# Batch 0 of a fused attention and MLP kernel: deferred pair sums, smaller last chunks, weights cast by their loads, the next batch's loads right behind them

## The chip, the cores and the metric

The kernel runs on one core of one Trainium2 chip. The metric is the device time of one execution in microseconds (us), as the median of several runs. A profiled execution spans some 2 us less than the time measured for it (772.4 against 774.1 for the kernel before); positions in time are from the start of that span. A load or a transpose has landed when the last of its 16 semaphore updates has come; all landings below are read from the trace's records of these updates.

## The reference

Four batches of q, k and v, each 6080 x 256 in fp32, tau = 1, then an MLP from 256 to 2048 and back:

```python
qn = q / (norm(q, axis=1) + 1e-06);  kn = k / (norm(k, axis=1) + 1e-06)
s = kn.transpose(0, 2, 1) @ qn / tau            # 256 x 256 for each batch
a = softmax(s)
x = (v @ a).reshape(B * N, 256)
out = gelu_tanh(x @ w_in) @ w_out               # w_in 256 x 2048, w_out 2048 x 256
```

Because `a` is small, the kernel multiplies it with w_in first (`aw`). A block of 512 rows of v then needs two products: `hp = aw^T v^T`, gelu, and `yp = g^T w_out`. Each batch has 12 blocks. While batch b's blocks run, the Gram matrix of batch b+1 is fed between them. Batch 0 has nothing to hide behind: its q and k come first, as fp32, and are cast and squared on chip.

## The kernel before

The order of the loads after batch 0's q and k, with the helpers that matter (cuts marked):

```python
first_chunks = chunks_of([2, 4, 6, 6, 6, 6, 6, 6, 3, 2])     # slots of 128 rows
for n, ch in enumerate(first_chunks):
    ...
    nc.vector.tensor_copy(qkb, st);  nc.scalar.activation(sqb, st, AF.Square)
    nc.vector.tensor_add(pair[:, :, 0:h], sqb[:, :, 0:h], sqb[:, :, h : 2 * h])
    ... gram(...), col_sums(...)
    stage_chunk(n + 4)
    if n == len(first_chunks) - 1:
        nc.gpsimd.tensor_copy(gate[:, 0:1], st[0:1, 1, 0, 0:1])   # GpSimd's loads wait here
...
def turn_v(nb):                       # v is needed transposed
    ...
    for s in range(n):
        nc.sync.dma_start_transpose(out=vT[:, :, s * 128 : s * 128 + 128], in_=t[:, s, :])
load_v(1)                             # GpSimd load, casts fp32 to bf16
for half in range(2):                 # w_in: fp32 by SyncE, cast on GpSimd
    ...
    nc.sync.dma_start(out=w[...], in_=win_v[...])
    nc.gpsimd.tensor_copy(win_bf[...], w[...])
for half in range(2):                 # w_out: likewise
    ...
for nb in (2, 3):
    load_v(nb)
...
# inside the loop over blocks
turn_v(nb + 2); load_v(nb + 4)
# on the first step of a batch's block 0: chunks 0 to 2 of the next batch, casting loads by GpSimd
```

In this text, v1 is block 1 of v in batch 0, and chunk (1,0) is the first chunk of q and k of batch 1.

Of the kernel before, what the change touches and what calls it, by code (L numbers as in the profile page):

```python
# [8 lines left out]
FP32 = mybir.dt.float32  # L9
# [9 lines left out]
def kernel(  # L19
# [10 lines left out]
    nc = tc.nc  # L30
# [13 lines left out]
    const = ctx.enter_context(tc.tile_pool(name="const", bufs=1))  # L44
    stage = ctx.enter_context(tc.tile_pool(name="stage", bufs=4))
    qkp = ctx.enter_context(tc.tile_pool(name="qkp", bufs=4))
    sqp = ctx.enter_context(tc.tile_pool(name="sqp", bufs=2))
    sq1 = ctx.enter_context(tc.tile_pool(name="sq1", bufs=4))
    accp = ctx.enter_context(tc.tile_pool(name="accp", bufs=2))
    smx = ctx.enter_context(tc.tile_pool(name="smx", bufs=2))  # L50
    awp = ctx.enter_context(tc.tile_pool(name="awp", bufs=2))
    vts = ctx.enter_context(tc.tile_pool(name="vts", bufs=4))
    gp = ctx.enter_context(tc.tile_pool(name="gp", bufs=2))
    yout = ctx.enter_context(tc.tile_pool(name="yout", bufs=3))
    vin = ctx.enter_context(tc.tile_pool(name="vin", bufs=5))

    pA = ctx.enter_context(tc.tile_pool(name="pA", bufs=2, space=bass.MemoryType.PSUM))
# [6 lines left out]



    def chunks_of(sizes):
        found, s0 = [], 0
        for n, size in enumerate(sizes):
            found.append((s0, size, n == 0))  # L70
            s0 += size
        assert s0 == S_ALL
        return found

    def load_chunk(eng, dst, b, chunk):
        s0, size, rem = chunk
        for x, src in enumerate((q, k)):
            eng.dma_start(  # L78
                out=dst[:, x, 0:size, :],
                in_=src[b, s0 * 128 : (s0 + size) * 128, :].rearrange("(p s) c -> p s c", s=size))  # L80
        if rem:
            for x, src in enumerate((q, k)):
                eng.dma_start(out=dst[:REM, x, size, :], in_=src[b, S_ALL * 128 : N, :])

    def slots_of(chunk):
        _, size, rem = chunk
        return [(s, 128) for s in range(size)] + ([(size, REM)] if rem else [])

    n_all = S_ALL + 1


    first_chunks = chunks_of([2, 4, 6, 6, 6, 6, 6, 6, 3, 2])
    staged = []

    def stage_chunk(n):
        if n < len(first_chunks):
            st = stage.tile([128, 2, SMAX, 256], FP32, tag="st", name="st")
            load_chunk(nc.sync, st, 0, first_chunks[n])
            staged.append(st)

    for n in range(4):
# [30 lines left out]
    def col_sums(cols, x, ones, first, last):  # L132

        for m in range(4):
            nc.tensor.matmul(  # L135
                cols[:, m : m + 1],
                lhsT=x[:, m // 2, m % 2 * 128 : m % 2 * 128 + 128],
                rhs=ones,
                start=first and m == 0,
                stop=last,  # L140
                skip_group_check=True,
            )
# [51 lines left out]

    G = pA.tile([128, 2, 256], FP32, tag="a", name="G")
    cols = pA.tile([128, 512], FP32, tag="a", name="cols")
    seen = 0
    for n, ch in enumerate(first_chunks):
        st = staged[n]
        size = ch[1]  # L200
        qkb = qkp.tile([128, 2, SMAX, 256], BF16, tag="qk", name="qkb")
        sqb = sqp.tile([128, 2, SMAX, 256], BF16, tag="sq", name="sqb")
        pair = sqp.tile([128, 2, SMAX // 2, 256], BF16, tag="pair", name="pair")
        for lo, hi, rows in [(0, size, 128)] + ([(size, size + 1, REM)] if ch[2] else []):
            nc.vector.tensor_copy(qkb[:rows, :, lo:hi], st[:rows, :, lo:hi])  # L205
            nc.scalar.activation(sqb[:rows, :, lo:hi], st[:rows, :, lo:hi], AF.Square)  # L206
        h = size // 2
        nc.vector.tensor_add(pair[:, :, 0:h], sqb[:, :, 0:h], sqb[:, :, h : 2 * h])  # L208
        for s, rows in slots_of(ch):
            gram(G, qkb, s, rows, seen == 0, seen == n_all - 1)  # L210
            seen += 1
        parts = [pair[:, :, s, :] for s in range(h)]
        if size % 2:
            parts.append(sqb[:, :, size - 1, :])
        if ch[2]:
            parts.append(sqb[:REM, :, size, :])
        for m, x in enumerate(parts):
            col_sums(cols, x, ones_bf[: x.shape[0], :],
                     n == 0 and m == 0, n == len(first_chunks) - 1 and m == len(parts) - 1)
        stage_chunk(n + 4)  # L220
        if n == len(first_chunks) - 1:
            nc.gpsimd.tensor_copy(gate[:, 0:1], st[0:1, 1, 0, 0:1])

    v0 = stage.tile([128, 2, SMAX, 256], FP32, tag="st", name="v0")
# [11 lines left out]
    def load_v(nb):  # L236
        if nb >= B * n_blocks:
            return
        r0, n, rest = v_parts(nb)
        t = vin.tile([128, 4, 256], BF16, tag="v", name="vb")  # L240
        nc.gpsimd.dma_start(  # L241
            out=t[:, 0:n, :],
            in_=v_rows[r0 : r0 + n * 128, :].rearrange("(p s) c -> p s c", s=n))
        if rest:
            nc.gpsimd.dma_start(out=t[:rest, n, :], in_=v_rows[r0 + n * 128 : r0 + n * 128 + rest, :])
        v_of[nb] = t

    def turn_v(nb):
# [8 lines left out]
            nc.sync.dma_start_transpose(out=vT[:, :, n * 128 : n * 128 + rest], in_=t[:rest, n, :])  # L257
        vT_of[nb] = vT

    load_v(1)  # L260

    def flat_stage(n, shape):
        w = stage.tile([128, 2, SMAX, 256], FP32, tag="st", name="wst")
        return w.rearrange("p a b c -> p (a b c)")[:, 0:2048].rearrange("p (c d) -> p c d", c=n)

    for half in range(2):
        w = flat_stage(2, None)
        for x in range(2):
            c0 = half * 1024 + x * 512
            nc.sync.dma_start(out=w[:, :, x * 512 : x * 512 + 512], in_=win_v[:, :, c0 : c0 + 512])  # L270
            nc.gpsimd.tensor_copy(win_bf[:, :, c0 : c0 + 512], w[:, :, x * 512 : x * 512 + 512])
    for half in range(2):
        w = flat_stage(8, None)
        nc.sync.dma_start(out=w, in_=wout_v[:, half * 8 : half * 8 + 8, :])
        nc.gpsimd.tensor_copy(wout_bf[:, half * 8 : half * 8 + 8, :], w)  # L275
    for nb in (2, 3):
        load_v(nb)


    r = smx.tile([128, 4], FP32, tag="r", name="r")  # L280
# [1 line left out]
    nc.scalar.activation(dummy, ones_f, AF.Exp)  # L282
    norms(r)
    Gs = scaled(G, r)
    vT0 = vts.tile([128, 2, 512], BF16, tag="vT", name="vT")
    vps = []
    for cc in range(2):
        p = pY.tile([128, 2, 256], FP32, tag="y", name="vps").rearrange("p a b -> p (a b)")
        for s in range(4):
            nc.tensor.matmul(p[:, s * 128 : s * 128 + 128],  # L290
                             lhsT=v0[:, s, cc * 128 : cc * 128 + 128],
                             rhs=ident, is_transpose=True)
        vps.append(p)
    T = turned(Gs)
    nc.scalar.activation(vT0[:, 0, :], vps[0], AF.Copy)
    nc.vector.tensor_copy(vT0[:, 1, :], vps[1])
    eT = smx.tile([128, 2, 256], BF16, tag="eT", name="eT")
    for jc in range(2):
        nc.scalar.activation(eT[:, jc, :], T[:, jc, :], AF.Exp, scale=r[:, jc : jc + 1])
    nc.scalar.activation(dummy, ones_f, AF.Gelu_apprx_tanh)  # L300
    rsinv = row_sums(eT)
    aw = awp.tile([128, 2, D], BF16, tag="aw", name="aw")
    wide = pH.tile([128, 2, 512], FP32, tag="h", name="wide")
    for ic in range(2):
        aw_part(eT, rsinv, aw, 0, ic, ps=wide[:, ic, :], act=ic == 1)
    aw_left = [(fs, ic) for fs in range(1, 4) for ic in range(2)]

    def more_aw(n):
        for _ in range(n):
            if aw_left:  # L310
                aw_part(eT, rsinv, aw, *aw_left.pop(0))

    more_aw(2)

    vT_of[0] = vT0
    turn_v(1)

    later_chunks = chunks_of([5, 6, 6, 6, 6, 6, 6, 6])

    def attention_steps(b, aw_next):  # L320

        loaded = []

        def load(n):
            if n < len(later_chunks):
                t = qkp.tile([128, 2, SMAX, 256], BF16, tag="qk", name="qkb")
                load_chunk(nc.gpsimd, t, b, later_chunks[n])
                loaded.append(t)

        for n in range(3):  # L330
            load(n)
        for _ in range(10):
            yield
        G = pA.tile([128, 2, 256], FP32, tag="a", name="G")
        acc = accp.tile([128, 2, 256], FP32, tag="acc", name="acc")
        seen = 0
        for n, ch in enumerate(later_chunks):
            load(n + 3)
            for s, rows in slots_of(ch):
                first, last = seen == 0, seen == n_all - 1  # L340
                gram(G, loaded[n], s, rows, first, last)
                flat = loaded[n][:rows, :, s, :]
                if first:
                    nc.vector.tensor_mul(acc, flat, flat)
                else:
                    sq = sq1.tile([128, 2, 256], BF16, tag="sq", name="sq")
                    nc.vector.tensor_mul(sq[:rows], flat, flat)  # L347
                    nc.vector.tensor_add(acc[:rows], acc[:rows], sq[:rows])  # L348
                seen += 1
                yield  # L350
                if seen % 4 == 0:
                    yield
# [42 lines left out]
    def y_part(st, s, fc0, fc1):  # L395
# [16 lines left out]
        if fc1 < FC:  # L412
            return
        if s == 0:
            st["ysb"] = yout.tile([128, 4, 256], FP32, tag="ysb", name="ysb")
        ysb = st["ysb"]
        r0 = b * N + blk * BLK
        if not (s % 2 == 1 or s == len(rows_of) - 1 or alone):
# [91 lines left out]
```

## Time and profile before

| | before |
|---|---|
| time, median of 3 runs | 774.2 us |
| TensorE busy | 740.1 us, 96% |
| last column sum of batch 0 ends | 39.0 us |
| block 0 starts (first `hp` product) | 46.0 us |
| block 1, block 2 start | 56.1, 79.1 us |
| TensorE waits over 0.3 us from block 1 on | 4.49 at chunk (1,0), 0.74 at block 2 |

The page's slices show TensorE full after the first tenth. The chain of waits tells which early event set the end, the timeline tells how long TensorE stood before an instruction and for whom (in square brackets), and the view of the DMA queues counts packets: q0 holds the loads that cast (GpSimd issues them), q1 the plain loads, stores and transposes. The lines themselves are in the prediction.

### The profile page before, as it was taken

To read this page: it belongs to the slowest core of one execution; us is meant where nothing else is said; L and a number is where in the kernel's file an instruction comes from. 1 tells how busy PE (TensorE), PEld (TensorE's weight loads), DVE (VectorE), ACT (ScalarE), POOL (GpSimd) and SP (SyncE) were. 2 spreads that over 40 slices of the span, in tenths; PEclk is the share of its full clock that TensorE was granted. 3 is DMA by queue.
4 is the path that set the end of the run, shared out by engine and by line. 5 is a ranking of instruction groups with operands and counts; after the bars stand their busy time and mean duration, and the time that the engine had idled before them with its cause. 6 is when DMAs were issued, how large, how long until landed. Compare 5 with 4: busy or idle time off the path is not lost.

```text
span 772.4 us, 12183 instructions
## 1 busy us (share of the span) xinstructions
PE 740.1 (96%) x5135; PEld 507.4 (66%) x5220; DVE 279.1 (36%) x485; ACT 421.3 (55%) x412; POOL 68.9 (9%) x121
## 2 busy tenths in 40 slices
PE   4787999999999999999999999999999999999998
PEld 2544666667666666667666666666667666666666
DVE  4732545453511555454431354545351101110011
ACT  5673555555555555555555555555545555555552
POOL 0052011001210002000300010100100000000000
PEclk9998999999999999999999999999999999999999
DMA  8999878323983466811794167732433333212111
GB/s 342 361 227 198 148 139 148 63 63 71 178 124 82 90 109 110 146 45 42 136 167 102 38 136 136 124 65 70 85 69 81 67 69 89 60 52 73 40 56 52
DMA packets 81751, 85.95 MB, mean 111 GB/s; under 512 B 56608, under 2 KB 60192, under 8 KB 81696
## 3 DMA queue, kind: packets, MB, share of 16 engines
q1 hardware_dynamic: 67216, 54.29, 25.8%
q0 software_dynamic: 14480, 30.87, 24.4%
q8 instruction: 41, 0.67, 0.4%
q14 instruction: 14, 0.11, 0.0%
HBM read 78.91 MB, written 24.90 MB: 134 GB/s over the span
## 4 chain that ended last, share of the span: by engine, by line
PE 88%; DMA 7%; ACT 1%; SPq 1%; issue 1%; POOL 0%; DVE 0%; ACTq 0%; POOLq 0%
PE yp L407 43%; PE hp L458 40%; PE G L123 4%; DMA st<-in_k_dram 3%; DMA vT<-vb 2%; DMA wst<-in_moe_w_out_dram 2%; ACT sqb L206 1%; PE ps L183 1%; SPq L255 1%; POOL wout_bf L275 0%; DMA vb<-in_v_dram 0%; SPq L78 0%; PE cols L135 0%; ACT g L462 0%; PE T L161 0%
## 5 line engine op out<-in xcount | busy, mean ns | idle before, releaser
L462 ACT ACTIVATE g<-hp 128x1024 bf16<-128x1024 f32 (+1 forms) x384 | 389.6, 1015 | 323.6 <-PE hp L458 314.9
L407 PE MATMUL yp<-wout_bf,g 128*128 128x256 bf16 (+1 forms) x3072 | 397.9, 273 | 0.7
L458 PE MATMUL hp<-vT,aw 128*128 128x512 bf16 (+1 forms) x1458 | 386.1, 378 | 5.0 <-DMA vT<-vb 0.7
L407 PEld LDWEIGHTS <-g 128*128 128x128 bf16 (+1 forms) x3072 | 301.2, 98 | 114.7 <-issue 3.3
L458 PEld LDWEIGHTS <-aw 128*128 128x128 bf16 x1536 | 150.1, 98 | 109.4 <-issue 6.2
L423 DVE COPY ysb<-yp 128x512 f32<-128x512 f32 (+1 forms) x93 | 64.0, 689 | 390.8 <-PE yp L407 390.8
L348 DVE TENSOR_TENSOR acc<-acc,sq 128x512 f32<-128x512 f32 (+1 forms) x141 | 97.6, 692 | 4.8
L123 PE MATMUL G<-qkb 128*128 128x256 bf16 (+1 forms) x384 | 75.6, 302 | 20.1 <-DVE qkb L205 15.7
L123 PEld LDWEIGHTS <-qkb 128*128 128x128 bf16 (+1 forms) x384 | 39.6, 107 | 29.2 <-DVE qkb L205 16.7
L347 DVE TENSOR_TENSOR sq<-qkb 128x512 bf16<-128x512 bf16 (+1 forms) x141 | 58.8, 417 | 0.0
L241 POOL DMA_DIRECT2D vb<-in_v_dram x47 | 26.2, 559 | 207.4 <-DMA vT<-vb 205.6
L192 DVE TENSOR_SCALAR aw<-ps,rsinv 128x512 bf16<-128x512 f32 x30 | 22.5, 750 | 29.0 <-PE ps L183 23.9
L78 POOL DMA_DIRECT2D qkb<-in_q_dram x24 | 13.2, 552 | 196.0 <-PE G L123 113.7
L206 ACT ACTIVATE sqb<-st 128x3072 bf16<-128x3072 f32 (+4 forms) x11 | 22.5, 2062 | 12.9 <-DMA st<-in_k_dram 8.8
L205 DVE CAST qkb<-st 128x3072 bf16<-128x3072 f32 (+4 forms) x11 | 14.6, 1330 | 8.7 <-DMA st<-in_k_dram 8.6
L183 PE MATMUL ps<-win_bf,eT 128*128 128x512 bf16 x54 | 17.3, 398 | 0.1
L358 POOL TENSOR_TENSOR r<-r,half 128x4 f32<-128x4 f32 x3 | 3.1, 1037 | 141.8 <-DVE r L357 141.8
L78 POOL DMA_DIRECT2D qkb<-in_k_dram x24 | 13.3, 555 | 1.4 <-DMA vb<-in_v_dram 1.4
L383 DVE RECIPROCAL den<-den 128x256 f32<-128x256 f32 x6 | 10.5, 1752 | 0.2
L427 DVE COPY ysb<-yp 64x256 f32<-64x256 f32 (+1 forms) x7 | 2.7, 415 | 21.2 <-PE yp L407 21.2
L208 DVE TENSOR_TENSOR pair<-sqb 128x1536 bf16<-128x1536 bf16 (+2 forms) x10 | 7.7, 767 | 7.0 <-ACT sqb L206 7.0
L183 PEld LDWEIGHTS <-eT 128*128 128x128 bf16 x64 | 6.2, 101 | 3.8 <-issue 1.9
(50 smaller groups left out, 63.4 us busy)
## 6 DMA issues: line engine op xcount, KB each, us to landing
out_dram<-ysb SPq DMA_DIRECT2D x44, 512.0 KB, 3.0
vb<-in_v_dram POOLq DMA_DIRECT2D x43, 256.0 KB, 5.5
qkb<-in_q_dram POOLq DMA_DIRECT2D x21, 384.0 KB, 6.1
qkb<-in_k_dram POOLq DMA_DIRECT2D x21, 384.0 KB, 7.7
st<-in_q_dram SPq DMA_DIRECT2D x6, 768.0 KB, 10.9
st<-in_k_dram SPq DMA_DIRECT2D x6, 768.0 KB, 13.0
vT<-vb SPq DMA_TRANSPOSE x188, 3.8
wst<-in_moe_w_in_dram SPq DMA_DIRECT2D x4, 512.0 KB, 6.5
```

What stands on the lines that cost most here:

```text
L78: eng.dma_start(out=dst[:, x, 0:size, :], in_=src[b, s0 * 128 : (s0 + size) * 128, :].rearrange("(p s) c -> p s c", s=size))
L123: nc.tensor.matmul(G[:, ic, :], lhsT=qk[:rows, 1, s, ic * 128 : ic * 128 + 128], rhs=qk[:rows, 0, s, :], start=first and ic == 0, stop=las ...
L183: nc.tensor.matmul(ps, lhsT=eT[:, jc, ic * 128 : ic * 128 + 128], rhs=win_bf[:, jc, fs * 512 : fs * 512 + 512], start=jc == 0, stop=jc == 1)
L192: nc.vector.tensor_scalar_mul(dst, ps, scale)
L206: nc.scalar.activation(sqb[:rows, :, lo:hi], st[:rows, :, lo:hi], AF.Square)
L241: nc.gpsimd.dma_start(out=t[:, 0:n, :], in_=v_rows[r0 : r0 + n * 128, :].rearrange("(p s) c -> p s c", s=n))
L347: nc.vector.tensor_mul(sq[:rows], flat, flat)
L348: nc.vector.tensor_add(acc[:rows], acc[:rows], sq[:rows])
L407: nc.tensor.matmul(yp[:rows, at, :], lhsT=g[:, fc, s * 128 : s * 128 + rows], rhs=wout_bf[:, fc, :], start=fc == 0, stop=fc == FC - 1)
L423: nc.vector.tensor_copy(ysb[:, s0 : s + 1, :], yp[:, 0 : s + 1 - s0, :])
L458: nc.tensor.matmul(hp[:, j, :cols], lhsT=aw[:, cc, fc * 128 : fc * 128 + 128], rhs=vT[:, cc, :cols], start=cc == 0, stop=cc == 1)
L462: nc.scalar.activation(g[:, 2 * i : 2 * i + 2, :cols], hp[:, :, :cols], AF.Gelu_apprx_tanh)
```

## The change

Its intent is to shorten the stretch before TensorE is full: keep the deferred sums out of the way of the casts, leave less work after the last chunk has landed, spare GpSimd the weights' casts, and have batch 1's loads start at once. The core of the diff (cut):

```diff
-    first_chunks = chunks_of([2, 4, 6, 6, 6, 6, 6, 6, 3, 2])
+    first_chunks = chunks_of([2, 5, 6, 6, 6, 6, 6, 4, 3, 2, 1], 7)   # 7: the chunk with the remainder
-            load_chunk(nc.sync, st, 0, first_chunks[n])
+            load_chunk((nc.sync, nc.scalar if n < 2 else nc.sync), st, 0, first_chunks[n])
...
+            if n >= n_chunks - 2:
+                nc.scalar.activation(sqb[:, 1, lo:hi], st[:, 1, lo:hi], AF.Square)
+                nc.vector.tensor_mul(sqb[:, 0, lo:hi], qkb[:, 0, lo:hi], qkb[:, 0, lo:hi])
...
+        if waiting is not None:
+            pairs_of(*waiting)          # the pair sums of the chunk before
...
-        if n == len(first_chunks) - 1:
+        if n == n_chunks - 3:
             nc.gpsimd.tensor_copy(gate[:, 0:1], st[0:1, 1, 0, 0:1])
...
-    load_v(1)
-    ... (w_in and w_out by SyncE into staging buffers, six casts on GpSimd)
-    for nb in (2, 3):
-        load_v(nb)
+    for fs in range(D // 512):
+        nc.gpsimd.dma_start(out=win_bf[:, :, fs * 512 : fs * 512 + 512],
+                            in_=win_v[:, :, fs * 512 : fs * 512 + 512])
+    load_v(1)
+    for half in range(2):
+        nc.gpsimd.dma_start(out=wout_bf[:, half * 8 : half * 8 + 8, :],
+                            in_=wout_v[:, half * 8 : half * 8 + 8, :])
+    for n in range(3):
+        load_qk(1, n)
+        if n < 2:
+            load_v(n + 2)
```

The first products of `aw` also move to two tiles, v0's transposes come later, and output blocks take buffers of the staging pool.

More of the change, by code (lines that the diff above doesn't have):

```diff
@@ L46 @@
     qkp = ctx.enter_context(tc.tile_pool(name="qkp", bufs=4))
-    sqp = ctx.enter_context(tc.tile_pool(name="sqp", bufs=2))
+    sqp = ctx.enter_context(tc.tile_pool(name="sqp", bufs=3))
+    prp = ctx.enter_context(tc.tile_pool(name="prp", bufs=2))
     sq1 = ctx.enter_context(tc.tile_pool(name="sq1", bufs=4))
@@ L53 @@
     gp = ctx.enter_context(tc.tile_pool(name="gp", bufs=2))
-    yout = ctx.enter_context(tc.tile_pool(name="yout", bufs=3))
     vin = ctx.enter_context(tc.tile_pool(name="vin", bufs=5))
@@ L63, with chunks_of @@
     SMAX = 6
-    def chunks_of(sizes):
+    def chunks_of(sizes, with_rem):
         found, s0 = [], 0
         for n, size in enumerate(sizes):
-            found.append((s0, size, n == 0))
+            found.append((s0, size, n == with_rem))
             s0 += size
@@ L73, in chunks_of, with load_chunk @@
         return found
-    def load_chunk(eng, dst, b, chunk):
+    def load_chunk(engines, dst, b, chunk):
         s0, size, rem = chunk
         for x, src in enumerate((q, k)):
-            eng.dma_start(
+            engines[x].dma_start(
                 out=dst[:, x, 0:size, :],
@@ L82, in load_chunk @@
             for x, src in enumerate((q, k)):
-                eng.dma_start(out=dst[:REM, x, size, :], in_=src[b, S_ALL * 128 : N, :])
+                engines[x].dma_start(out=dst[:REM, x, size, :], in_=src[b, S_ALL * 128 : N, :])
     def slots_of(chunk):
@@ L89 @@
     n_all = S_ALL + 1
-    first_chunks = chunks_of([2, 4, 6, 6, 6, 6, 6, 6, 3, 2])
+    first_chunks = chunks_of([2, 5, 6, 6, 6, 6, 6, 4, 3, 2, 1], 7)
+    TAIL = 7
     staged = []
@@ L196, with sums_of, pairs_of @@
     cols = pA.tile([128, 512], FP32, tag="a", name="cols")
-    seen = 0
+    n_chunks = len(first_chunks)
+    seen, summed = 0, 0
+    def sums_of(parts, last):
+        nonlocal summed
+        for m, x in enumerate(parts):
+            col_sums(cols, x, ones_bf[: x.shape[0], :], summed == 0, last and m == len(parts) - 1)
+            summed += 1
+    def pairs_of(n, sqb):
+        size = first_chunks[n][1]
+        h = size // 2
+        pair = prp.tile([128, 2, SMAX // 2, 256], BF16, tag="pair", name="pair")
+        nc.vector.tensor_add(pair[:, :, 0:h], sqb[:, :, 0:h], sqb[:, :, h : 2 * h])
+        parts = [pair[:, :, s, :] for s in range(h)]
+        if size % 2:
+            parts.append(sqb[:, :, size - 1, :])
+        sums_of(parts, False)
+    waiting = None
     for n, ch in enumerate(first_chunks):
@@ L202 @@
         sqb = sqp.tile([128, 2, SMAX, 256], BF16, tag="sq", name="sqb")
-        pair = sqp.tile([128, 2, SMAX // 2, 256], BF16, tag="pair", name="pair")
         for lo, hi, rows in [(0, size, 128)] + ([(size, size + 1, REM)] if ch[2] else []):
             nc.vector.tensor_copy(qkb[:rows, :, lo:hi], st[:rows, :, lo:hi])
-            nc.scalar.activation(sqb[:rows, :, lo:hi], st[:rows, :, lo:hi], AF.Square)
-        h = size // 2
-        nc.vector.tensor_add(pair[:, :, 0:h], sqb[:, :, 0:h], sqb[:, :, h : 2 * h])
+            if n >= n_chunks - 2:
+                nc.scalar.activation(sqb[:, 1, lo:hi], st[:, 1, lo:hi], AF.Square)
+                nc.vector.tensor_mul(sqb[:, 0, lo:hi], qkb[:, 0, lo:hi], qkb[:, 0, lo:hi])
+            else:
+                nc.scalar.activation(sqb[:rows, :, lo:hi], st[:rows, :, lo:hi], AF.Square)
         for s, rows in slots_of(ch):
@@ L211 @@
             seen += 1
-        parts = [pair[:, :, s, :] for s in range(h)]
-        if size % 2:
-            parts.append(sqb[:, :, size - 1, :])
-        if ch[2]:
-            parts.append(sqb[:REM, :, size, :])
-        for m, x in enumerate(parts):
-            col_sums(cols, x, ones_bf[: x.shape[0], :],
-                     n == 0 and m == 0, n == len(first_chunks) - 1 and m == len(parts) - 1)
+        if waiting is not None:
+            pairs_of(*waiting)
+            waiting = None
+        if n < TAIL:
+            waiting = (n, sqb)
+        else:
+            sums_of([sqb[:rows, :, s, :] for s, rows in slots_of(ch)], n == n_chunks - 1)
         stage_chunk(n + 4)
-        if n == len(first_chunks) - 1:
+        if n == n_chunks - 3:
             nc.gpsimd.tensor_copy(gate[:, 0:1], st[0:1, 1, 0, 0:1])
@@ L258, in turn_v, with load_qk @@
         vT_of[nb] = vT
+    later_chunks = chunks_of([5, 6, 6, 6, 6, 6, 6, 6], 0)
+    loaded_of = {}
+    def load_qk(b, n):
+        if b < B and n < len(later_chunks):
+            t = qkp.tile([128, 2, SMAX, 256], BF16, tag="qk", name="qkb")
+            load_chunk((nc.gpsimd, nc.gpsimd), t, b, later_chunks[n])
+            loaded_of[b, n] = t
+    for fs in range(D // 512):
+        nc.gpsimd.dma_start(out=win_bf[:, :, fs * 512 : fs * 512 + 512],
+                            in_=win_v[:, :, fs * 512 : fs * 512 + 512])
     load_v(1)
-    def flat_stage(n, shape):
-        w = stage.tile([128, 2, SMAX, 256], FP32, tag="st", name="wst")
-        return w.rearrange("p a b c -> p (a b c)")[:, 0:2048].rearrange("p (c d) -> p c d", c=n)
     for half in range(2):
-        w = flat_stage(2, None)
-        for x in range(2):
-            c0 = half * 1024 + x * 512
-            nc.sync.dma_start(out=w[:, :, x * 512 : x * 512 + 512], in_=win_v[:, :, c0 : c0 + 512])
-            nc.gpsimd.tensor_copy(win_bf[:, :, c0 : c0 + 512], w[:, :, x * 512 : x * 512 + 512])
-    for half in range(2):
-        w = flat_stage(8, None)
-        nc.sync.dma_start(out=w, in_=wout_v[:, half * 8 : half * 8 + 8, :])
-        nc.gpsimd.tensor_copy(wout_bf[:, half * 8 : half * 8 + 8, :], w)
-    for nb in (2, 3):
-        load_v(nb)
+        nc.gpsimd.dma_start(out=wout_bf[:, half * 8 : half * 8 + 8, :],
[4 more added lines that the diff above has]
+            load_v(n + 2)
     r = smx.tile([128, 4], FP32, tag="r", name="r")
@@ L284 @@
     Gs = scaled(G, r)
-    vT0 = vts.tile([128, 2, 512], BF16, tag="vT", name="vT")
-    vps = []
-    for cc in range(2):
-        p = pY.tile([128, 2, 256], FP32, tag="y", name="vps").rearrange("p a b -> p (a b)")
-        for s in range(4):
-            nc.tensor.matmul(p[:, s * 128 : s * 128 + 128],
-                             lhsT=v0[:, s, cc * 128 : cc * 128 + 128],
-                             rhs=ident, is_transpose=True)
-        vps.append(p)
     T = turned(Gs)
-    nc.scalar.activation(vT0[:, 0, :], vps[0], AF.Copy)
-    nc.vector.tensor_copy(vT0[:, 1, :], vps[1])
     eT = smx.tile([128, 2, 256], BF16, tag="eT", name="eT")
@@ L299 @@
         nc.scalar.activation(eT[:, jc, :], T[:, jc, :], AF.Exp, scale=r[:, jc : jc + 1])
+    vT0 = vts.tile([128, 2, 512], BF16, tag="vT", name="vT")
+    vps = pH.tile([128, 2, 512], FP32, tag="h", name="vps")
+    for cc in range(2):
+        for s in range(4):
+            nc.tensor.matmul(vps[:, cc, s * 128 : s * 128 + 128],
+                             lhsT=v0[:, s, cc * 128 : cc * 128 + 128],
+                             rhs=ident, is_transpose=True)
+        nc.scalar.activation(vT0[:, cc, :], vps[:, cc, :], AF.Copy)
     nc.scalar.activation(dummy, ones_f, AF.Gelu_apprx_tanh)
@@ L302, with aw_product @@
     aw = awp.tile([128, 2, D], BF16, tag="aw", name="aw")
-    wide = pH.tile([128, 2, 512], FP32, tag="h", name="wide")
+    def aw_product(fs, ic, pool=pA, tag="a"):
+        ps = pool.tile([128, 512], FP32, tag=tag, name="ps")
+        for jc in range(2):
+            nc.tensor.matmul(
+                ps,
+                lhsT=eT[:, jc, ic * 128 : ic * 128 + 128],
+                rhs=win_bf[:, jc, fs * 512 : fs * 512 + 512],
+                start=jc == 0, stop=jc == 1)
+        return ps
+    ps0 = [aw_product(0, ic, pY, "y") for ic in range(2)]
+    for lo in (0, 256):
+        for ic in range(2):
+            nc.vector.tensor_scalar_mul(aw[:, ic, lo : lo + 256], ps0[ic][:, lo : lo + 256],
+                                        rsinv[:, ic : ic + 1])
     for ic in range(2):
-        aw_part(eT, rsinv, aw, 0, ic, ps=wide[:, ic, :], act=ic == 1)
-    aw_left = [(fs, ic) for fs in range(1, 4) for ic in range(2)]
+        aw_part(eT, rsinv, aw, 1, ic)
+    aw_left = [(fs, ic) for fs in range(2, 4) for ic in range(2)]
     def more_aw(n):
@@ L311, in more_aw @@
                 aw_part(eT, rsinv, aw, *aw_left.pop(0))
-    more_aw(2)
     vT_of[0] = vT0
     turn_v(1)
-    later_chunks = chunks_of([5, 6, 6, 6, 6, 6, 6, 6])
     def attention_steps(b, aw_next):
-        loaded = []
-        def load(n):
-            if n < len(later_chunks):
-                t = qkp.tile([128, 2, SMAX, 256], BF16, tag="qk", name="qkb")
-                load_chunk(nc.gpsimd, t, b, later_chunks[n])
-                loaded.append(t)
-        for n in range(3):
-            load(n)
+        if b > 1:
+            for n in range(3):
+                load_qk(b, n)
         for _ in range(10):
@@ L337, in attention_steps @@
         for n, ch in enumerate(later_chunks):
-            load(n + 3)
+            load_qk(b, n + 3)
+            qk = loaded_of.pop((b, n))
             for s, rows in slots_of(ch):
                 first, last = seen == 0, seen == n_all - 1
-                gram(G, loaded[n], s, rows, first, last)
-                flat = loaded[n][:rows, :, s, :]
+                gram(G, qk, s, rows, first, last)
+                flat = qk[:rows, :, s, :]
                 if first:
@@ L414, in y_part @@
         if s == 0:
-            st["ysb"] = yout.tile([128, 4, 256], FP32, tag="ysb", name="ysb")
+            ysb = stage.tile([128, 2, SMAX, 256], FP32, tag="st", name="ysb")
+            st["ysb"] = ysb.rearrange("p a b c -> p (a b) c")
         ysb = st["ysb"]
```

## The prediction

> **What bounds the kernel now.** I read the page first, for which engine is full and where it is not:
>
> ```profile
> PE   4787999999999999999999999999999999999998
> PEclk9998999999999999999999999999999999999999
> DMA  8999878323983466811794167732433333212111
> ...
> PE 88%; DMA 7%; ACT 1%; SPq 1%; issue 1%; POOL 0%; DVE 0%; ACTq 0%; POOLq 0%
> ```
>
> TensorE is full from about the fifth slice (77 us) to the end; only the first tenth has room, and the DMA engines are busy there. Next I listed TensorE's waits of over 0.25 us: after 79.14 us there is none. So the time is the moment when block 2 of batch 0 starts (79.14) plus 695 us of unbroken matrix work that the change leaves alone, and the change can act only on that moment. What sets it is in the chain of waits (in order of time, cut to this stretch):
>
> ```profile
> 55.16 3.64 DMA vb<-in_v_dram
> 58.80 0.02 issue
> 58.82 2.15 SPq L255
> 60.97 0.04 issue
> 61.02 1.31 SPq L255
> 62.33 0.04 issue
> 62.38 1.32 SPq L255
> 63.69 0.04 issue
> 63.74 15.27 DMA vT<-vb
> 79.01 0.14 issue
> 79.14 0.38 PE hp L458
> ```
>
> Block 2 waits for its transposed v: v block 2 lands at 58.80, its four DMA transposes land only at 79.01. The timeline of TensorE shows two waits ahead of it, a large one that attracts the eye and a small one that counts:
>
> ```profile
> 65.93 0.61 PE L123 MATMUL G<-qkb 128*128 128x256 bf16 x2 [4.49 <-DMA qkb<-in_k_dram]
> ...
> 79.14 1.02 PE L458 MATMUL hp<-vT,aw 128*128 128x512 bf16 x3 [0.74 <-DMA vT<-vb]
> ```
>
> Had the 4.49 us wait for batch 1's first q/k chunk vanished, TensorE would have stood longer at the second. Why are transposes that small so slow? The queues between 66 and 78 us:
>
> ```profile
> q0 software_dynamic: 878, 2.27, 96.1%
> q1 hardware_dynamic: 877, 0.20, 13.2%
> ```
>
> The counts are equal: each small transpose packet (16 engines x 12 us x 13.2% / 877 = 29 ns) is followed on its engine by one large packet of a casting load (16 x 12 x 96.1% / 878 = 210 ns). One v block takes 4 x 256 packets of 256 bytes, 64 on each engine, so 64 alternations: some 15 us while the casting queue has work.
>
> **What the Trainium skill says.** "DMA: Bandwidth & Descriptors", section "Queues, rings and completion order": an SDMA engine takes turns between its queue rows, a packet at a time. The 878 against 877 agree. The same page, "SWDGE vs HWDGE vs iDMA": a DMA that casts must come from GpSimd, so casting the weights in their loads puts them on the queue of batch 1's loads, while transposes stay on the other kind. The trace agrees: all casting loads are on q0, all transposes on q1. "TensorE: Matmul & The Clock Gate", Part 1, "What's actually happening": the clock falls to half after an idle window of about 3.4 us and comes back after a busy one. Here: after the 4.49 us wait the clock records show 0.5 until 71.12, so 5.2 us at half speed, 2.6 us lost.
>
> **The change part by part.**
>
> (1) First chunks. The q/k loads are bound by the transfers: six-slot chunks land 3.78 us apart (12.43, 16.21, 20.00, 23.78 by the trace's landing records), 1.573 MB at 416 GB/s. The compute chain of a chunk, square 2.76 and pair sum 0.96 plus handovers, happens to be 3.78 too, so deferring the sums shortens the chain to 2.8 but the transfers still pace it. What is gained: the remainder's two issues (0.57 and 0.59) leave the start and k goes by a second issuer, so the engines are full sooner; they were 77% busy between 2 and 4 us, 0.5 us saved. The last chunk lands at 35.77 and the last column sum ends at 38.93, 3.2 us later. With tail chunks of 3, 2 and 1 slots, half of each of the last two squares on VectorE and no pair sums, I work from the last landing at 35.3 backwards at 0.41 MB/us: the 4-slot chunk with the remainder lands at 31.5, the 3-slot at 33.4, the 2-slot at 34.6. ScalarE then squares until 34.1 (1.91 + 0.63), 35.6 (1.47) and, with half chunks, 36.2 and 36.7. VectorE has a deferred pair sum (0.96) in between and ends its cast and product of the last slot near 37.0; its sums end at 37.4. Gain 1.5 us.
>
> (2) From the last sum to block 0: 7.1 us now (38.93 to 46.01). The two products into one tile cost a wait of 1.06 us for VectorE; two tiles take it away. The transposes of v and the narrower scalings are about even. Block 0 starts near 43.5, 2.5 us earlier. But block 0's own start is not what sets 79.14.
>
> (3) Casting queue. Six casts on GpSimd (4 x 1.04 and 2 x 1.90 us) and the wait of the batch 1 loads behind them go: POOL issued its first v load at 36.32 and the next at 55.16. Now everything is in one queue, in this order: w_in, v1, w_out, chunk (1,0), v2, chunk (1,1), v3, chunk (1,2), then v4, v5, chunk (1,3), v6. Times of one packet on an engine from the trace's packet records: 512 bytes 59 ns, 2,048 bytes 173, 2,560 bytes 210, 3,072 bytes 247; so 1,024 bytes about 98 by the line through them. Packets on each engine up to v2: w_in 64 x 98 = 6.3 us; v1 8 x 173 = 1.4; w_out 128 x 59 = 7.55; chunk (1,0) 16 x 210 for its q and k of five slots and 8 x 59 for the remainder's 128 rows, 3.8; v2 1.4. Sum 20.4, and 64 packets of v1's transposes between them at 31 ns, 2.0: 22.4 us. Start: the gate now waits for the 3-slot chunk, cumulated 11.67 MB; by the landings (11.14 MB at 32.47, 11.93 MB at 34.44) that is 33.8, less the 0.5, so 33.3, and 33.9 after the 0.55 us copy. The first casting load now moves its first packet 3.8 us after its issue (36.32 to 40.16), later ones 1.3 us (55.16 to 56.42); q/k and v0 still fill the engines to about 36.5. I take 37.2 (36.5 to 37.8). Then v2's last packet is at 59.6 and v2 lands at 60.0, against 58.80: a little later. The engines' idle time is used now (the windows show DMA 1% busy from 54 to 56.4 and 51% from 34 to 38), but v2, which led its group, now stands behind chunk (1,0), and the weights come in smaller packets.
>
> (4) v2's transposes. First packet now 4.7 us after v2's landing (58.80 to 63.5): 64.7. By then chunk (1,1) and nearly all of v3 are through; behind lie 16 + 8 + 8 + 16 + 8 = 56 packets per engine (chunk (1,2), v4, v5, chunk (1,3), v6): 32 x 247 + 24 x 173 = 12.05 us, with 56 transposes at 31 ns 13.8, then 8 alone, 14.0 in all. So 78.7, landed 78.9. The same sum for the kernel before (64 packets of chunk (1,0)'s rest onwards: 13.4 + 2.0 from 63.5) gives 78.85 against the measured 79.01, so I trust it to about 1 us, beside the 1 us of the start.
>
> (5) TensorE meanwhile. Chunk (1,0) lands near 58 instead of 65.88, so the first wait shrinks or goes, and TensorE reaches block 2 about 10 to 12 us later, at 68 to 71. There it stands for some 8 to 10 us for v2. The large wait moves to the small one's place, and half clock comes with it: 2.6 us, which the kernel before also paid, but ahead of a wait that hid them; here they lie behind the last wait.
>
> Sum: start of block 2 at 79.0 instead of 79.14, -0.1; half clock after it +2.6; everything later unchanged, since TensorE has no other wait (output buffers move to a pool with four slots, which no row waits for). 774.2 - 0.1 + 2.6 = 776.7; I say 776.5.
>
> **The rivals.** A: the loads of q/k are the bound, as the largest wait says. Then block 2 starts at 69 to 70 and the time falls by some 9 to 10 us, to about 764.5. For it: 4.49 us is the longest wait. Against it: transposes alternate with loads, and the new order gives them no quieter time. B: a middle course, if the casting queue runs dry between 60 and 75 (its issues wait for earlier landings: after 59.40 POOL waited 0.90, 1.42, 0.98 and 1.55 us) or starts sooner; each us without casting packets saves about that much, and a wait under 3 us would spare the half clock: 768 to 774. C: GpSimd needs much longer to issue w_out's 1,024 runs per load than the 0.54 us that 128 runs take; then everything behind slides, 779 to 785. No row shows such a load now, so I can't exclude it. D: a full win on every count, without waits (block 0 at 43.5, ten us for it, eight groups of 1.85): block 2 at 68.5, still only -1.4%.
>
> **Range and chances.** Two terms, start of the casting queue and alternation, give +-2 us about 776.5; A and B pull below, C above. 768 to 780.5 for 8 in 10. Even D stays inside 2% (758.7), and slower by 2% would need 15 us: faster 0.02, same 0.965, slower 0.015.
>
> **What would show it.** The last long wait of TensorE should be at block 2, for the transposed v, 6 us or more, near 79 us, with half clock behind it; the wait for chunk (1,0) under 3 us; the last column sum near 37.4; block 0 near 43.5; q0 and q1 with equal packet counts between 66 and 76. It is wrong if v2's transposes land before about 74, if the wait at block 2 is gone, or if a wait after it appears.

## The result, and the profile after

The changed kernel took 776.99 us (776.50 to 777.25, 4 runs) against 774.27 us (773.95 to 774.89, 4 runs). The ratio is 1.0033, with a 95% interval from 1.0016 to 1.0051: a little slower, within 2%. Ratios here are the mean time of one kernel's runs over that of the other's of the same rounds, so not quite the ratio of the medians.

The page of the changed kernel, its parts 2 and 4:

```profile
PE   4776999999999999999999999999999999999998
PEclk9987999999999999999999999999999999999999
DMA  9999568412983365721695167723432333212111
...
PE 90%; DMA 6%; SPq 1%; issue 1%; ACT 1%; POOL 0%; DVE 0%; ACTq 0%; DVEq 0%
```

TensorE is full again from the fifth slice on, so the loss lies ahead of that. The granted clock is 0.8 and 0.7 in the third and fourth slices, where before it was 0.9 and 0.8. The chain of waits between 30 and 66 us (start, length, what):

```profile
33.34 0.17 POOL gate L243
33.50 3.53 POOL win_bf L291 x4
37.03 9.48 DMA vb<-in_v_dram
46.51 0.02 issue
46.53 1.29 SPq L276
...
50.44 14.06 DMA vT<-vb
64.49 0.14 issue
64.63 1.44 PE hp L484 x3
```

It has the shape of the chain before, but for another block: v1 is loaded behind w_in and lands at 46.51, and its four transposes have landed at 64.49. Before, v1 was loaded first, and block 1 didn't wait for it. The timeline of TensorE confirms the place:

```profile
64.63 1.44 PE L484 MATMUL hp<-vT,aw 128*128 128x512 bf16 x3 [10.08 <-DMA vT<-vb]
```

Line 484 is the `hp` product; this one is the first of block 1. The wait of 4.49 us for chunk (1,0) is gone (its q and k landed at 54.91 and 56.72), and so is the 0.74 us at block 2. One wait of 10.08 us stands in for both. The queues of the changed kernel between 56 and 64 us show why 256 KB take that long:

```profile
q0 software_dynamic: 606, 1.48, 97.5%
q1 hardware_dynamic: 590, 0.13, 14.8%
```

606 packets of casting loads and 590 of transposes: turn by turn. Windows right after the wait show the price in clock (the columns are the busy time of each engine, then the granted clock, the DMA share and GB/s):

```profile
64.60:69.00 4.40, 4.15 (x14) 2.19 (x16) 0.00 (x0) 1.02 (x1) 0.53 (x1) 0.50 1.11 202
69.00:80.00 11.00, 10.95 (x79) 7.63 (x78) 3.77 (x7) 6.01 (x6) 0.00 (x0) 1.00 1.22 123
```

4.4 us at half speed are 2.2 us lost. How this comes to the difference: block 2's first gelu starts at 80.26 us before and at 82.86 after, 2.6 us later, and what follows it takes 692.1 and 692.3 us. Block 1 started some 8.6 us later than before (56.07 to 64.63). Gone are 4.49 + 2.6 (half clock) + 0.74 us of waits between block 1 and block 2; come in is 2.2 us of half clock. 8.6 - 7.8 + 2.2 = 3.0, close to the 2.6 seen.

### The profile page after: what moved, and what is told of

Read it like the earlier page. It is cut to its first block, busy times and chain, and to the rows that moved or that the text cites. A ratio compares the mean times of both kernels' runs of the same rounds, so it can differ in the third digit from the quotient of the medians.

```text
span 775.2 us, 12214 instructions
## 1 busy us (share of the span) xinstructions
PE 739.3 (95%) x5155; PEld 507.8 (66%) x5240; DVE 277.9 (36%) x487; ACT 420.9 (54%) x413; POOL 65.2 (8%) x121
## 4 chain that ended last, share of the span: by engine, by line
PE 90%; DMA 6%; SPq 1%; issue 1%; ACT 1%; POOL 0%; DVE 0%; ACTq 0%; DVEq 0%
PE yp L432 44%; PE hp L484 41%; PE G L124 4%; DMA st<-in_k_dram 3%; DMA vT<-vb 2%; DMA vb<-in_v_dram 1%; PE ps L184 1%; SPq L276 0%; POOL win_bf L291 0%; ACT sqb L230 0%; SPq L78 0%; PE cols L136 0%; ACT g L488 0%; PE T L162 0%; DVE qkb L225 0%
## 5 line engine op out<-in xcount | busy, mean ns | idle before, releaser
L124 PE MATMUL G<-qkb 128*128 128x256 bf16 (+1 forms) x384 | 74.0, 296 | 14.9 <-DVE qkb L225 14.9
L230 ACT ACTIVATE sqb<-st 128x3072 bf16<-128x3072 f32 (+5 forms) x10 | 21.1, 2123 | 10.6 <-DMA st<-in_k_dram 10.6
L225 DVE CAST qkb<-st 128x3072 bf16<-128x3072 f32 (+6 forms) x12 | 14.6, 1225 | 15.0 <-DMA st<-in_k_dram 15.0
L212 DVE TENSOR_TENSOR pair<-sqb 128x1536 bf16<-128x1536 bf16 (+2 forms) x7 | 5.8, 836 | 0.0
```

The lines of the kernel that those rows point to most:

```text
L124: nc.tensor.matmul(G[:, ic, :], lhsT=qk[:rows, 1, s, ic * 128 : ic * 128 + 128], rhs=qk[:rows, 0, s, :], start=first and ic == 0, stop=las ...
L230: nc.scalar.activation(sqb[:rows, :, lo:hi], st[:rows, :, lo:hi], AF.Square)
```

## The experiments

Theory A: a block starts when its four transposes have taken their 64 turns on each DMA engine, and while casting loads are queued each turn costs one of their packets. The position of a v block in the casting queue, and what stands behind it, decide. Rivals: the casting queue is late as a whole, in any order (B); there was only the one wait, and nothing stands behind it (C); the transposes are slow by themselves; the half clock is the cost.

All runs that follow gave right results. Their times stand beside those of the kernel before on the same chip.

### v1 ahead of w_in

```diff
+    load_v(1)
     for fs in range(D // 512):
         nc.gpsimd.dma_start(out=win_bf[...], in_=win_v[...])
-    load_v(1)
```

> v block 1 loaded ahead of the four w_in loads instead of behind them; nothing else. Theory A (alternation: a block starts when its four transposes have taken their 64 turns per engine with the casting loads' packets): v1 lands near 38.5 instead of 46.5, its transposes move from about 42.5 beside the small packets of w_in (98 ns) and w_out (60 ns), 64 x some 105 ns, and end before 51; the 10.1 us wait at block 1 goes. But v block 2 still lands near 60.5 behind chunk (1,0), its transposes then alternate with 247 and 172 ns packets and end at 74 to 78; TensorE is at block 2 at about 69.5 and waits there 5 to 8 us, half clock behind it: start of block 2 77 to 80.5 (counting the half clock) against 81.7 in the changed kernel, time 773 to 776. Rival B (the casting queue as a whole is late, whatever alternates): the order within it changes little, time 776 to 777.5 and the long wait stays at block 1. Rival C (one wait only, at block 1): it goes and nothing replaces it, 765 to 767.

Measured: 774.49 us against 774.37, ratio 1.0005 (0.9991 to 1.0019). The first wait went and a second appeared at block 2, in the timeline of TensorE:

```profile
77.69 1.89 PE L484 MATMUL hp<-vT,aw 128*128 128x512 bf16 x4 [6.78 <-DMA vT<-vb]
```

v1's transposes had landed at 51.16 us. The half clock behind block 2 ran to 80.68. The place of the wait, its length and the time are what A named. C falls (765 to 767), and so does B.

### v1 and v2 ahead of w_in

```diff
+    load_v(1)
+    load_v(2)
     for fs in range(D // 512):
         nc.gpsimd.dma_start(out=win_bf[...], in_=win_v[...])
-    load_v(1)
...
     for n in range(3):
         load_qk(1, n)
-        if n < 2:
-            load_v(n + 2)
+        if n == 1:
+            load_v(3)
```

> v blocks 1 and 2 both loaded ahead of the w_in loads. Theory A: both blocks' transposes alternate with the small packets of w_in and w_out and have landed by about 56; no wait of TensorE over 3 us after block 0, no half clock after 50 us, block 2 starts near 70: time 765 to 768, faster than both kernels. w_in comes 2.8 us later, which may cost up to 1 us ahead of block 0. Rival B: the same bytes stand in the queue, so the long wait moves to the weights or to chunk (1,0), 5 us or more, and the time stays at 774 to 778.

Measured: 767.66 us against 774.37, ratio 0.992 (0.9907 to 0.9934). No long wait was left in batch 0's first blocks; v2's transposes had landed at 57.95 us, and block 2's first gelu started at 71.47 us, 11.4 us earlier than in the changed kernel. The bytes in the queue are the same, so B falls. Its profile has waits of 0.83 and 2.34 us near 117 and 133 us that nobody expected. The kernel was run again later, with another one:

> the kernel with v1 and v2 first once more, on the same chip as the candidate, for a fair comparison and to see whether the two late waits near 117 and 133 us belong to it: 767 to 768.5; if the waits are gone in this profile they were of that execution, and the profiled time is 2 to 3 us less than the 769.06 of that one.

Measured: 767.83 us against 774.73, ratio 0.9915 (0.9901 to 0.993). This profile has no wait of TensorE over 0.25 us between 55 and 300 us, and its execution was shorter than that profiled first (whose 769.06 us was the longest of its four runs). So the late waits belonged to that execution; why it had them stays open.

### Casting loads held back until v1's transposes have landed

v1 keeps its place and its landing time; only the company of its transposes changes.

```diff
-    for n in range(3):               # chunk (1,0) and what follows it
-        ...
     turn_v(1)
+    nc.gpsimd.tensor_copy(gate[:, 1:5], vT_of[1][0:1, 0, 0:512:128])   # one element of each transpose
+    for n in range(3):
+        ...
```

> the changed kernel with chunk (1,0) and all loads behind it held back by GpSimd until the four transposes of v block 1 have landed; v1 itself lands at the same 46.5. Theory A: only w_out's 60 ns packets are left to alternate with, then nothing: the transposes land by 56 instead of 64.5, block 1 starts at about 55 to 56; chunk (1,0) then lands near 60 and v block 2 near 62, whose transposes end near 77 to 79, so the long wait goes to block 2 and the time is 773 to 778. Rival (the transposes are slow by themselves, in issue or in the transfer): they land at 60 or later though nothing alternates with them, and block 1 still starts after 62.

Measured: 777.39 us against 774.37, ratio 1.0046 (1.0031 to 1.0061). v1 landed at 45.97 us, its transposes at 52.82, where the changed kernel's had landed at 64.49. The queues of this kernel between 49 and 52 us:

```profile
q1 hardware_dynamic: 1132, 0.26, 110.6%
q0 software_dynamic: 292, 0.14, 35.3%
```

1,132 packets of the transposes' queue in 3 us, against 590 in 8 us in company. They aren't slow by themselves. Block 1 started without a wait, and the long one went to block 2 once more, as the timeline shows:

```profile
80.34 1.89 PE L485 MATMUL hp<-vT,aw 128*128 128x512 bf16 x4 [9.99 <-DMA vT<-vb]
```

Holding loads back makes the one block early and the next late: the time is no better, in the range that was expected. It is the clearest evidence for A, and it shows why a gain at one wait doesn't arrive.

### The half clock alone

TensorE was given products that nobody reads in place of its idle time ahead of block 1.

```diff
+            if nb == 1:
+                warm = pA.tile([128, 512], FP32, tag="a", name="warm")
+                for _ in range(42):      # 34 in the second run
+                    nc.tensor.matmul(warm, lhsT=win_bf[:, 0, 0:128], rhs=win_bf[:, 0, 0:512], ...)
```

> the changed kernel with 42 matrix products of 512 columns, whose result nobody reads, put ahead of block 1, where TensorE waits 10.1 us (42 x 0.216 = 9.1 us). It takes the half clock away and leaves the wait. If the half clock after the wait costs what the clock record says (4.4 us at half, 2.2 us lost): 774.8, that is 2.2 us or 0.28% less than the changed kernel, with block 1 starting at the same 64.6. If it costs nothing of its own: 777.0. If the products push block 1 back: over 777.

Measured: 776.79 us against 774.37, ratio 1.0034 (1.0021 to 1.0046), which looks like the changed kernel. But in this execution block 0 ended later (the clock had been at half until 47.75 us), the products ended near 66 us, and block 1 was pushed back to 65.98. So the run decides nothing, and it was repeated with fewer products:

> as the run with 42 products, with 34 (7.5 us), since the 42 ended at 66.1 in that run and pushed block 1 back past the landing of its transposes. Now they end by 62 to 64 whenever block 0 ends (54.5 to 56.1), block 1 starts at 63.2 to 64.7 with the landing, after an idle time under 3 us and at full clock. If the half clock costs 2.2 us of its own: time 774.5 to 775.3, block 2 some 15.0 us after block 1 instead of 16.3 (by the first gelu of each), 1 us more at the first group. If it costs nothing: 777.

Measured: 774.73 us against 774.15, ratio 1.0012 (0.9999 to 1.0024). The timeline of TensorE:

```profile
55.16 7.50 PE L482 MATMUL warm<-win_bf 128*128 128x512 bf16 x33
64.53 1.02 PE L489 MATMUL hp<-vT,aw 128*128 128x512 bf16 x4 [1.87 <-DMA vT<-vb]
```

(One of the 34 records is missing.) Block 1 starts with the landing, as in the changed kernel, but at full clock (the clock record shows no half clock after 46.53 us), and block 2's first gelu comes 15.0 us after block 1's instead of 16.3, as expected for a half clock with a cost of its own. The time is 2.3 us less than the changed kernel's by the medians, and 1.6 us less by the two ratios. So the half clock costs about 2 us of its own, and it isn't the whole loss: block 1 still starts 8.5 us later than in the kernel before.

### The first phase alone

The kernel before with the new chunk sizes, deferred sums, shared last squares, two issuers and output buffers from the staging pool, and nothing else; the gate stays at the last chunk.

```diff
-    first_chunks = chunks_of([2, 4, 6, 6, 6, 6, 6, 6, 3, 2])
+    first_chunks = chunks_of([2, 5, 6, 6, 6, 6, 6, 4, 3, 2, 1], 7)
... (the loop over the first chunks as changed, but)
-        if n == n_chunks - 3:
+        if n == n_chunks - 1:
```

> the kernel before with the first part of the change alone: chunk sizes, pair sums one chunk behind, the last squares shared, two issuers for the first loads, output buffers from the staging pool; weights by the old loads and GpSimd casts, gate at the last chunk, loads of batch 1 as before. Theory A: the last column sum ends at about 36.9 instead of 38.93, and every later step, the weights' staging, their casts and the load of v block 2 behind them, follows from it, so block 2 starts 1.5 to 2 us earlier: 772.2 to 772.9. Rival: the first phase is hidden behind the loads, 774.3.

Measured: 774.12 us against 774.15, ratio 0.9998 (0.9985 to 1.0011). The expected gain of 1.5 to 2 us did not come; the time is the one that the rival named. The timelines show that the load of v2 is no earlier. First the kernel before:

```profile
35.37 2.88 SPq L270 DMA_DIRECT2D wst<-in_moe_w_in_dram  x4
...
55.16 1.61 POOL L241 DMA_DIRECT2D vb<-in_v_dram  x3
```

Then this kernel:

```profile
35.22 2.04 SPq L291 DMA_DIRECT2D wst<-in_moe_w_in_dram  x4
...
55.89 1.60 POOL L262 DMA_DIRECT2D vb<-in_v_dram  x3
```

The first of the weights' staging loads starts at the same time, and the last one, of w_out, even later: at 41.26 us against 39.93. By the program it takes over the buffer of v0, and in both traces it starts as TensorE's transposes of v0 end (41.23 and 39.90 us). It lands at 54.01 against 53.28, and v2's load follows 0.7 us later too. In this execution the granted clock was at half until 42.42 us, so its last column sum ended at 39.4, not at 36.9 us, and the transposes of v0 came behind that. The profile therefore doesn't show what the first phase does at full clock. The five runs (773.44 to 774.76 us) show no gain, and why none of them has it stays open.

### The casting queue alone

The kernel before with the weights cast by their loads and the loads of batch 1 right behind, in the changed kernel's order, and nothing else.

```diff
-    load_v(1)
-    ... (w_in, w_out by SyncE, casts on GpSimd; v2, v3)
+    ... (w_in, v1, w_out, chunk (1,0), v2, chunk (1,1), v3, chunk (1,2), all casting loads)
```

> the kernel before with the third part of the change alone: weights cast by their loads, v1 behind w_in, chunk (1,0) ahead of v2; first phase, products and gate as before. Theory A: the gate opens 2.4 us later than in the changed kernel (35.8 against 33.3), so v1 lands near 48.5 to 49 and its transposes near 66 to 67; block 1 waits for them 9 to 11 us and starts at 66 to 67: time 778.5 to 779.5, slower than the changed kernel by the 2 us that the first phase saves. Rival (the casting loads are a gain, and another part costs the time): 770 to 774.

Measured: 778.76 us against 774.15, ratio 1.0064 (1.005 to 1.0079), as A expected. v1 landed at 48.87 us, its transposes had landed at 66.90, and TensorE waited 11.94 us at block 1:

```profile
67.15 1.44 PE L452 MATMUL hp<-vT,aw 128*128 128x512 bf16 x3 [11.94 <-DMA vT<-vb]
```

So this part is what costs the time, and the rest of the change wins back 0.3% of it (1.0064 to 1.0033): the gate opens earlier, and v1 lands at 46.51 instead of 48.87.

### The kernel before, v2 loaded ahead of the weights' casts

```diff
     load_v(1)
+    load_v(2)
...
-    for nb in (2, 3):
-        load_v(nb)
+    load_v(3)
```

> the kernel before with one line moved: v block 2 is loaded right behind v block 1, ahead of the weights' casts on GpSimd, instead of behind them. Theory A: its transposes have landed by about 60, while the casting queue is empty or nearly so; the 0.74 us wait at block 2 goes and with v2 out of its way chunk (1,0) lands 1.4 us earlier, at 64.5, which then sets the pace: block 2 at 77.0, time 772.0 to 772.5. Rival (v2's landing is not what block 2 waits for): 774.3.

Measured: 771.29 us against 774.15, ratio 0.9962 (0.9949 to 0.9974). v2's transposes had landed at 64.16 instead of 79.01 us and the wait at block 2 went, so v2 was what the kernel before waited for in the end. The time is 0.7 us below the range expected, and the inner working was partly wrong: the transposes had not landed by about 60, and the k of chunk (1,0) landed at 65.75 us, no earlier than before, so TensorE still waited for it:

```profile
65.80 0.61 PE L123 MATMUL G<-qkb 128*128 128x256 bf16 x2 [4.67 <-DMA qkb<-in_k_dram]
```

The remaining gain of the profiled execution is in the clock: half speed held until 68.44 us here, until 71.12 before.

### A better order

From v1 and v2 first: w_in's first quarter goes ahead of them, v3 moves ahead of chunk (1,1), and v0's two halves get a tile each.

```diff
-    load_v(1)
-    load_v(2)
     for fs in range(D // 512):
+        if fs == 1:
+            load_v(1)
+            load_v(2)
         nc.gpsimd.dma_start(out=win_bf[...], in_=win_v[...])
...
-        if n == 1:
+        if n == 0:
             load_v(3)
...
-    vps = pH.tile([128, 2, 512], FP32, tag="h", name="vps")
     for cc in range(2):
+        vps = pH.tile([128, 2, 512], FP32, tag="h", name="vps")
```

> v1 and v2 behind the first of the four w_in loads (so the first product need not wait for them), v3 ahead of chunk (1,1), and the two halves of v0's transposes in a tile each, so the second half doesn't wait 0.7 to 1.0 us for ScalarE's copy of the first. Theory A: as with v1 and v2 first, no long wait after block 0; block 0 starts 0.5 to 1 us earlier, and since nothing waits behind it that comes through whole: 766.3 to 767.5 against 767.7. If another wait takes it up (v's later blocks, as the 0.8 and 2.3 us waits near 117 and 133 us in that run's profile): 767 to 769.

Measured: 765.81 us against 774.73, ratio 0.9884 (0.9868 to 0.9901), 0.5 us below the range expected, the best of all and better than both kernels; the version it starts from took 767.83 us in the same rounds. Who TensorE waited for from 36 to 300 us (total, times, longest):

```profile
PE T L162 <- DVE Gs L154: 1.4, 1, 1.4
PE ps L184 <- DMA win_bf<-in_moe_w_in_dram: 1.0, 1, 1.0
PE hp L486 <- ACT g L490: 0.4, 2, 0.2
PE ps L329 <- issue: 0.2, 1, 0.2
```

No wait for a transposed v is left. A wait of 1.0 us for w_in is new. The profiled execution was the longest of this kernel's four (767.12 us) and hardly earlier at block 0: its first gelu starts at 48.51 us, with the clock at half until 48.31, and at 48.90 in the profile of the version it starts from. So the profile doesn't show the 2 us by which the median is ahead, and which of the three edits brings them is open.

All profiles together bear out the frame of the prediction. The time from block 2's first gelu to the end of the span is 692.0 to 692.3 us in every kernel but three, so that start is what counts. In two of the three, v1 first and v1's transposes undisturbed, half clock still ran for 1.0 and 1.7 us after that gelu:

| kernel | block 2's first gelu | rest of the span | longest wait from block 1 to block 2 |
|---|---|---|---|
| before | 80.26 | 692.1 | 4.49, chunk (1,0) |
| changed | 82.86 | 692.3 | 10.08, block 1 |
| v1 first | 79.67 | 692.9 | 6.78, block 2 |
| v1, v2 first | 71.47 | 695.8 (late waits, 3.2) | none |
| v1, v2 first, again | 73.39 | 692.3 | none |
| v1's transposes undisturbed | 82.33 | 693.2 | 9.99, block 2 |
| busy TensorE, 42 | 82.09 | 692.3 | none |
| busy TensorE, 34 | 80.63 | 692.3 | 1.87, block 1 |
| first phase alone | 80.35 | 692.0 | 4.41, chunk (1,0) |
| casting queue alone | 84.84 | 692.0 | 11.94, block 1 |
| before, v2 early | 77.99 | 692.1 | 4.67, chunk (1,0) |
| better order | 73.00 | 692.3 | none |

## Why the prediction was right or wrong

The time was right, 776.5 against 776.99, and so was the reason in kind: the loads' lateness was not the bound, transposes alternate with casting packets, and a long wait for a transposed v with half clock behind it takes the place of the 4.49 us wait. The place was wrong, by one block, and the agreement to 0.5 us owes something to chance. By a sign that I had named myself, that the wait at block 2 is gone, this picture of where TensorE stands was wrong.

The step that failed is in part (3): "64 packets of v1's transposes between them at 31 ns, 2.0". I let v1's transposes start as v1 landed and run beside w_out's small packets. In part (4) I gave v2's transposes the 4.7 us from landing to first packet that I had read from the trace, but v1's none. They too needed 4.0 us (46.51 to 50.52), and by then most of w_out was through (2,008 of its 2,048 packets). 64 turns beside chunk (1,0), v2 and chunk (1,1) took 14.0 us from the first packet to the landing at 64.49. So block 1 waited. The 2.0 counts only what these packets cost the casting queue; when they end, and that block 1 stands waiting for them, the prediction never worked out.

Part (4) came out nearly as worked out: v2's transposes moved their first packet at 64.42 us (64.7 worked out) and landed at 78.44 (78.9). Block 2 didn't wait because TensorE, held up at block 1, came to it only at 81.74. Two things in that agreement are luck. The 4.7 us were misread: in the kernel before v2's first transpose packet moved at 62.78, not 63.5, so 4.0 us after v2's landing. And the turns went as I had assumed only up to 73 us (569 packets of q0 and 575 of q1 from 66 to 73). From 74 to 77 us only 26 casting packets were moved, yet the transposes' packets took a median of 0.26 us each instead of 31 ns; what held them back there, no run shows.

Both pictures give nearly the same start of block 2, one set by v2's transposes and the other by v1's. Mine: 79.0 and 2.6 us of half clock, 81.6. The chip's: block 1 at 64.63, 2.2 us of half clock, block 1's products, and 81.74. With v1 moved ahead of w_in the chip shows my picture, a 6.78 us wait that ends at 77.69. That kernel took 774.5 us, 2 us less than the 776.5 that I had worked out for such a wait: it ended 1.3 us sooner, and the half clock behind it lasted 3.0 us instead of 5.2.

Point by point:

- Part (1): last column sum near 37.4; measured 36.9. Right.
- Part (2): block 0 near 43.5; measured 45.29. The clock was at half from 38.28 to 45.10, which I had not counted, and v0's second half waited 0.69 us for ScalarE's copy from the tile they share.
- Part (3): first casting packet at 37.2; measured 35.94. v2 landed at 60.55; worked out 60.0. The term for v1's transposes is the one told above.
- Part (5): chunk (1,0) near 58; its k landed at 56.72. Its wait went, as said. The half clock after the long wait: 2.6 expected, 2.2 by the clock record, about 2 by the experiment.
- The prediction's own rivals: its A (the loads are the bound) would have given 764.5 and didn't come. Its middle course B (768 to 774) didn't come either. Its C, a slow issue of w_out on GpSimd, is refuted: the two loads took 1.79 us to issue.

## What to carry to other kernels

When small transposes and large loads share the DMA engines, load what has to be transposed first, so that its transposes meet small packets or none: here the same bytes in another order (v1 and v2 first) made the change 0.8% faster than before instead of 0.3% slower, and 1.2% with the further edits of the last experiment. Removing the longest wait of a profile pays only down to the next wait behind it, so work out the second before counting on the first. And a wait that moves next to the unbroken part of a kernel also brings its clock penalty where nothing hides it.

## What the Trainium skill lacked or had wrong

- "DMA: Bandwidth & Descriptors", "Queues, rings and completion order", says that engines take turns between queue rows by packets, and the runs agree (606 packets against 590). It lacks what that does to transposes: a 512-row block took 3.9 us from its first packet to its landing in company of w_out's last 512-byte packets (48.91 to 52.82 us) and 14.0 us beside the loads of q, k and v (50.52 to 64.49).
- The same page, "Specifications", gives a first-byte latency of about 0.6 us for the sync path and 1 us for the GpSimd path. Here the first transpose packet moved 4.0 us after the issue began (46.53 to 50.52) under load and 2.9 us in the quieter run (45.99 to 48.91); the first casting load's first packet moved 2.5 us (33.45 to 35.94) and 3.8 us (36.32 to 40.16) after its issue began, with other loads in flight. With the engines idle it was 1.2 us (55.16 to 56.40, kernel before), near the page's figure.
- "TensorE: Matmul & The Clock Gate", "What's actually happening": the window of about 3.4 us and its free phase agree with the records (half clock for 3.4, 6.8 and 10.2 us). It says that the free phase makes runs of one kernel differ. What it lacks is the size of that scatter in time while products are sparse: one and the same kernel (v1 and v2 first), in two executions on two chips, was at half clock from 34.59 to 38.00 and 41.41 to 44.83 us in one execution and from 30.90 to 47.97 in the other, and block 0's first gelu came at 46.62 and 48.90 us.
